# A state-space layer with gated feed-forward, forward and backward: gates by token rows, spectra formed in place, doubled table buffers, a shared transform pool, and another order and pace of the table chain

## Chip, core and metric

The kernel runs on one core of a Trainium2 chip. The metric is the device time of one execution in microseconds (us). "Span" is the profiled execution; it is some 2 us shorter than the time reported for it.

## The reference, cut

```python
def fwd(u, A, B, C, log_dt, Dskip, w1, w2):       # u: 2048 tokens x 512 channels, bf16
    xn = layernorm(u)
    dt = exp(log_dt)                              # per channel
    K  = einsum("dn,dnl,dn->dl", C, exp(dt*A*l), dt*B).real   # 128 states, complex; a kernel of 2048 taps per channel
    s  = irfft(rfft(pad(xn)) * rfft(pad(K)))[:2048] + xn * Dskip
    g  = silu(silu(xn @ w1) @ w2)                 # feed-forward 512 -> 1792 -> 512
    return u + s * g
# the outputs: fwd(...) and its gradients with respect to the 11 inputs, for a given grad_out
```

The channels are worked in four blocks of 128. For each block a *table* stage forms K (powers of exp(dt A) as sine times magnitude: E, Y, W, then ps_k, Xr, ps_e, KE). The code and the recorded texts count blocks from zero, so their "third block" is the fourth here. Long transforms are matmuls in two steps with a transposed load between: step one (ps_s from xn, Kb or ds, evacuated to dA), a transposing load dB<-dA, step two (ps_s from dB).

## The kernel before: the parts concerned

The kernel has generators that issue a few instructions and yield; a weaver takes steps from several in turn. So the place of a `yield` largely sets the order of instructions in every engine's queue (the build can still move one, as run 9 will show). The queues run in that order: compared by source line, VectorE ran its 1147 instructions of the kernel before, ScalarE its 673, and SP issued its 298 transfers, in the order of the built program.

```python
def dft_fwd(k, w8, U, X, ev):
    A = w8.tile(..., name="dA", tag="w8")
    ...                                    # step one: 32 matmuls, four evacuations to A
    yield
    B = w8.tile(..., name="dB", tag="w8")
    nc.sync.dma_start_transpose(B, A)      # the transposing load
    yield                                  # ONE step between issue and use
    ...                                    # step two: 16 matmuls on B, evacuated to a third tile X

def gen_conv_fwd(k, b):
    Kb = dft.tile(..., name="Kb", tag="t4")
    nc.sync.dma_start(Kb, k.Kd[b])         # the table stage's KE, back from memory; no step before its use
    yield from dft_fwd(k, dft, Kb, KX, k.evc)
    ...                                    # product with U, inverse transform, S_b
# gate (by 128-channel blocks), six operations on VectorE for each half block:
        nc.vector.tensor_scalar(out=th, in0=th, scalar1=-0.5, scalar2=0.5, ...)
        nc.vector.tensor_single_scalar(out=sl, in_=g, scalar=-1.0, op=ALU.add)
        ...
        nc.sync.dma_start(k.dSd[b][:, cs], fl(ds))      # d s goes to memory and back
# the program:
    def chain():
        yield from woven([gen_tables(k, 0), gen_conv_x(k, 0)], [5, 1])
        for b in range(1, 4):
            yield from woven([gen_tables(k, b), chained([gen_conv_fwd(k, b - 1), gen_conv_x(k, b)])], [3, 2])
    interleave_until([gen_ffn_fwd(k)], [1], ch)         # one chain step for each feed-forward step
    ...
    run(ch)                                             # what is left of the chain, alone
    fwd3 = gen_conv_fwd(k, 3); next(fwd3); run(pre(3)); run(fwd3); run(pre(0))
    interleave([gen_conv_bwd(k, 0), chained([post(0), pre(1), post(1), pre(2), post(2)])], [1, 2])
    interleave([chained(gen_conv_bwd(k, b) for b in range(1, 4)), gen_ffn_da(k, da)], [1, 2])
    interleave([gen_ssm_bwd(k, sb), chained([gen_dw2(k, fw), gen_dw1(k, fw)]), after(8, gen_ln_bwd(k, fw))], [2, 1, 1])
```

Of the kernel before, what the change touches and what calls it, by code (L numbers as in the profile page):

```python
# [18 lines left out]
PH = 1 << 18  # L19
# [67 lines left out]
def interleave_until(gens, weights, other):  # L87

    gens, weights = list(gens), list(weights)
    while gens:  # L90
        for i in range(len(gens) - 1, -1, -1):
            for _ in range(weights[i]):
                try:
                    next(gens[i])
                except StopIteration:
                    gens.pop(i); weights.pop(i)
                    break
        next(other, None)
# [15 lines left out]
def make_consts(k, wp):  # L114
# [24 lines left out]
    for h in range(2):  # L139
        hs = slice(8 * h, 8 * h + 8)  # L140
        prod = wp.tile([P, 8, 128], I32, name="prod", tag="prod", bufs=2)
        TT(out=prod[:], in0=il[:, hs].unsqueeze(2).to_broadcast([P, 8, 128]),
           in1=jf[:].unsqueeze(1).to_broadcast([P, 8, 128]), op=ALU.mult)
        ks = wp.tile([P, 8, 2, 128], I32, name="ks", tag="ks", bufs=2)
        TS(out=ks[:, :, 1, :], in_=prod[:], scalar=8191, op=ALU.bitwise_and)
        TS(out=prod[:], in_=prod[:], scalar=6144, op=ALU.add)
        TS(out=ks[:, :, 0, :], in_=prod[:], scalar=8191, op=ALU.bitwise_and)
        nc.scalar.activation(out=k.TF[:, hs], in_=ks[:], func=ACT.Sin, scale=2.0 * math.pi / 8192.0, bias=k.mpi[:])
# [112 lines left out]

def dft_fwd(k, w8, U, X, ev):

    nc, pc = k.nc, k.pc
    A = w8.tile([P, 2, 16, 16, 8], BF16, name="dA", tag="w8")
    for h in range(2):
        for c in range(2):
# [3 lines left out]
            ev(A[:, c, :, 8 * h:8 * h + 8, :], ps[:].rearrange("p t (g e) -> p g t e", e=8))  # L271
    yield
    B = w8.tile([P, 2, 16, P], BF16, name="dB", tag="w8")
    nc.sync.dma_start_transpose(B[:].rearrange("p c g k -> p (c g) k"), A[:].rearrange("p c g t e -> p (c g t e)"))
    yield
    F2 = k.F2
    for h in range(2):
        for c, (m0, m1) in enumerate(((0, 1), (2, 0))):
# [5 lines left out]
            ev(X[:, c, 8 * h:8 * h + 8, :], ps[:])  # L284


def dft_inv(k, w8, Y, ev, consume):
    nc, pc = k.nc, k.pc
    A2 = w8.tile([P, 2, 16, P], BF16, name="dA2", tag="w8")
# [17 lines left out]
def cplx_mul(k, w8, out, a, b, conj=False):  # L307
    nc = k.nc
    TT = nc.vector.tensor_tensor
    n = 8  # L310
    for g0 in range(0, 16, n):
        gs = slice(g0, g0 + n)
        t2 = w8.tile([P, 2, n, P], BF16, name="cm2", tag="cm2")
        TT(out=out[:, :, gs], in0=b[:, :, gs], in1=a[:, 0:1, gs].to_broadcast([P, 2, n, P]), op=ALU.mult)
        TT(out=t2[:, 0], in0=b[:, 1, gs], in1=a[:, 1, gs], op=ALU.mult)
        TT(out=t2[:, 1], in0=b[:, 0, gs], in1=a[:, 1, gs], op=ALU.mult)
        TT(out=out[:, 0, gs], in0=out[:, 0, gs], in1=t2[:, 0], op=ALU.add if conj else ALU.subtract)
        TT(out=out[:, 1, gs], in0=out[:, 1, gs], in1=t2[:, 1], op=ALU.subtract if conj else ALU.add)
# [22 lines left out]
def ssm_magnitudes(k, wp, S, ldt):  # L341
# [7 lines left out]
    nc.vector.scalar_tensor_tensor(out=ph[:], in0=k.dt[:], scalar=PH / (2 * math.pi), in1=S["Ai"], op0=ALU.mult, op1=ALU.mult)  # L349
    nc.vector.tensor_copy(out=qa_out(k.tau[:]), in_=qa_in(ph[:]))  # L350
    mag = wp.tile([P, 4, NE + len(Y_EXP), P], BF16, name="mag_all")
    for i, e in enumerate(E_EXP + Y_EXP):
        nc.scalar.activation(out=mag[:, :, i], in_=lamr[:].rearrange("p (b d) -> p b d", b=4), func=ACT.Exp, scale=float(e))
    for b in range(4):
# [23 lines left out]
def gen_tables(k, b):  # L378
# [4 lines left out]
    mag = tbl.tile([P, NX, P], BF16, name="mag", tag="mag")  # L383
    nc.sync.dma_start(mag[:].rearrange("p e d -> p (e d)"), k.Md[b])
    Xr = tbl.tile([P, 32, NE, 4], BF16, name="Xr", tag="Xr")
    for h in range(2):
        hs = slice(b * P + 64 * h, b * P + 64 * h + 64)
        ms = slice(64 * h, 64 * h + 64)
        E = tbl.tile([P, 2, 16, NE, 4], BF16, name="E", tag="E")
        Y = tbl.tile([P, 2, 16, 32, 4], BF16, name="Y", tag="Y")  # L390
        H = tbl.tile([P, 2, 16, 3, 4], BF16, name="H", tag="H")
        nc.gpsimd.memset(Y[:, 0, :, 0, :], 1.0)
        nc.gpsimd.memset(Y[:, 1, :, 0, :], 0.0)
        qe = lambda ap: ap.rearrange("p e (q a) -> p e q a", a=4)
        for (x0, n) in ((0, 8), (8, 8), (16, 5), (21, 7), (28, 3)):
# [4 lines left out]
            TS(out=V[:, 1, 0:n], in_=V[:, 1, 0:n], scalar=PH - 1, op=ALU.bitwise_and)  # L400
            TS(out=V[:, 0, 0:n], in_=V[:, 1, 0:n], scalar=PH // 4, op=ALU.add)
            TS(out=V[:, 0, 0:n], in_=V[:, 0, 0:n], scalar=PH - 1, op=ALU.bitwise_and)  # L402
            sn = tbl.tile([P, 2, 8, 64], BF16, name="sn", tag="ts", bufs=2)
            nc.scalar.activation(out=sn[:, :, 0:n], in_=V[:, :, 0:n], func=ACT.Sin, scale=-2 * math.pi / PH, bias=k.pi[:])  # L404
            for c in range(2):
# [4 lines left out]
                for o, s0, s1 in segs:  # L410
                    TT(out=o.rearrange("p q e a -> p e q a"), in0=qe(sn[:, c, s0:s1]), in1=qe(mag[:, x0 + s0:x0 + s1, ms]), op=ALU.mult)
# [14 lines left out]
        for q0 in range(0, 16, 8):  # L426
            W = tbl.tile([P, 4, 8, NE, 4], BF16, name="W", tag="W")
# [21 lines left out]
    KE = tbl.tile([P, 8, 8, 32], BF16, name="KE", tag="W")  # L449
# [31 lines left out]
def gen_conv_x(k, b):  # L481
# [3 lines left out]
    k.U = dft.tile([P, 2, 16, P], BF16, name="U", tag="w8")  # L485
    yield from dft_fwd(k, dft, lambda t: k.xn[:, t, bs], k.U, k.evc)
    k.nc.sync.dma_start(k.Ud[b], k.U[:].rearrange("p c g k -> p (c g k)"))
# [3 lines left out]
def gen_conv_fwd(k, b):  # L491
# [3 lines left out]
    U = k.U  # L495
    Kb = dft.tile([P, 4, 16, 32], BF16, name="Kb", tag="t4")
    nc.sync.dma_start(Kb[:].rearrange("p a t q -> p a (t q)"), k.Kd[b].rearrange("a i (r s) x -> (i r) a (s x)", s=2))
    KX = dft.tile([P, 2, 16, P], BF16, name="KX", tag="w8")
    yield from dft_fwd(k, dft, lambda t: Kb[:, :, t, :], KX, k.evc)
    nc.sync.dma_start(k.KXd[b], KX[:].rearrange("p c g k -> p (c g k)"))  # L500
    yield
    YX = dft.tile([P, 2, 16, P], BF16, name="YX", tag="w8")
    cplx_mul(k, dft, YX, KX, U)
    S = dft.tile([P, 16, P], BF16, name="S_b", tag="t4")

    def consume(t0, n, ps):
        xd = dft.tile([P, 8, P], BF16, name="xd", tag="xd")
        nc.vector.tensor_tensor(out=xd[:], in0=k.xn[:, t0:t0 + n, bs], in1=k.Dbc[:, bs].unsqueeze(1).to_broadcast([P, n, P]), op=ALU.mult)
        nc.vector.tensor_tensor(out=S[:, t0:t0 + n], in0=ps[:], in1=xd[:], op=ALU.add)
        if b in k.gate:  # L510
            gate_post(k, b, t0 // 8, S[:, t0:t0 + n])
    yield from dft_inv(k, dft, YX, k.evc, consume)
    if b not in k.gate:
        nc.sync.dma_start(k.Sd[b], S[:].rearrange("p t d -> p (t d)"))
# [4 lines left out]
def gen_ffn_fwd(k):  # L519
    nc, fp = k.nc, k.fp  # L520
    D, FT, DK, T = k.D, k.FT, k.DK, k.T
    for c in range(T // 2):
# [5 lines left out]
        for f in range(FT // 2):  # L528
            if f in (0, 4):
                hT = fp.tile([P, 8, 256], BF16, name="hT", tag="hT", bufs=3)  # L530
# [13 lines left out]
        ob = fp.tile([P, 4, 2, P], BF16, name="ob", tag="ob", bufs=2)  # L544
        for t in range(2):
# [4 lines left out]
            k.evf(ob[:, :, t, :], ps[:].rearrange("p (b d) -> p b d", b=4))  # L550
            yield
        k.st(k.Od[:, :, cs].rearrange("b p n -> p b n"), ob[:].rearrange("p b t d -> p b (t d)"))
# [3 lines left out]
def gen_gate_pre(k, b, pool):  # L556
# [3 lines left out]
    bs = slice(b * P, b * P + P)  # L560
    k.gate[b] = []
    for h in range(2):
        ts = slice(8 * h, 8 * h + 8)
        cs = slice(1024 * h, 1024 * h + 1024)
        n = dict(g=4, th=2, G=2, ds=1)
        g, th, G, ds = (pool.tile([P, 8, P], BF16, name=nm, tag=nm, bufs=n[nm]) for nm in ("g", "th", "G", "ds"))
        fl = lambda t: t[:].rearrange("p t d -> p (t d)")
        nc.sync.dma_start(fl(th), k.Od[b][:, cs])
        nc.sync.dma_start(G[:], k.g_v[:, ts, bs])
        x = None  # L570
        if b == 3:
            x = pool.tile([P, 8, P], BF16, name="x3", tag="x3", bufs=2)
            nc.sync.dma_start(x[:], k.x_v[:, ts, bs])
        nc.scalar.activation(out=g[:], in_=th[:], func=ACT.Silu)
        nc.scalar.activation(out=th[:], in_=th[:], func=ACT.Tanh, scale=0.5)
        TT(out=ds[:], in0=G[:], in1=g[:], op=ALU.mult)
        nc.sync.dma_start(k.dSd[b][:, cs], fl(ds))

        nc.vector.tensor_scalar(out=th[:], in0=th[:], scalar1=-0.5, scalar2=0.5, op0=ALU.mult, op1=ALU.add)
        sl = k.do[:, ts, bs]  # L580
        nc.vector.tensor_single_scalar(out=sl, in_=g[:], scalar=-1.0, op=ALU.add)
        TT(out=th[:], in0=sl, in1=th[:], op=ALU.mult)
        nc.vector.tensor_single_scalar(out=th[:], in_=th[:], scalar=1.0, op=ALU.add)
        TT(out=sl, in0=th[:], in1=G[:], op=ALU.mult)
        k.gate[b].append((g, x))
# [3 lines left out]
def gate_post(k, b, h, S, x=None):  # L589
# [3 lines left out]
    bs = slice(b * P, b * P + P)  # L593
    ts = slice(8 * h, 8 * h + 8)
    g, x3 = k.gate[b][h]
    x = x or x3
    TT(out=k.do[:, ts, bs], in0=k.do[:, ts, bs], in1=S, op=ALU.mult)
    TT(out=g[:], in0=g[:], in1=S, op=ALU.mult)
    TT(out=x[:], in0=x[:], in1=g[:], op=ALU.add)
    k.st(k.o0_v[:, ts, bs], x[:])  # L600


def gen_gate_post(k, b, pool):
    for h in range(2):
        S = pool.tile([P, 8, P], BF16, name="S", tag="S", bufs=1)
        x = pool.tile([P, 8, P], BF16, name="x", tag="x", bufs=1)
        k.nc.sync.dma_start(S[:].rearrange("p t d -> p (t d)"), k.Sd[b][:, 1024 * h:1024 * h + 1024])
        k.nc.sync.dma_start(x[:], k.x_v[:, 8 * h:8 * h + 8, b * P:b * P + P])
        gate_post(k, b, h, S[:], x)
# [3 lines left out]
def gen_conv_bwd(k, b):  # L613
# [3 lines left out]
    ds = dft.tile([P, 16, P], BF16, name="ds_b", tag="ds")  # L617
    nc.sync.dma_start(ds[:].rearrange("p t d -> p (t d)"), k.dSd[b])
    DS = dft.tile([P, 2, 16, P], BF16, name="DS", tag="w8")
    yield from dft_fwd(k, dft, lambda t: ds[:, t, :], DS, k.evc)  # L620
# [4 lines left out]
    GX = dft.tile([P, 2, 16, P], BF16, name="KGX", tag="w8")  # L625
    cplx_mul(k, dft, GX, U, DS, conj=True)

# [454 lines left out]
```

## Time and profile before

823.46 us, median of three runs (822.28 to 825.41). I follow a kernel by marks in the trace, each the start of an instruction:

| mark (us from the start) | before |
|---|---|
| last ps_o (end of the feed-forward forward) | 245.7 |
| last step-one matmuls from Kb (fourth block: all tables done) | 327.8 |
| first ps_da (feed-forward backward begins) | 377.9 |
| last ps_dx (feed-forward backward ends) | 575.0 |
| first matmul of G (gradients of the state space begin) | 586.7 |
| last psS (their last sums) | 778.6 |
| end of the span | 820.7 |

The page's strips, the stages, the waits and the thin stretch are shown in the prediction.

### The profile page before, as it was taken

The page shows a single profiled execution, that of the slowest core. Times are in us where ns is not written, and L with a number is a line of the kernel's source. Part 1 is how long each engine was busy: PE and PEld are TensorE (multiplying, and loading weights), DVE is VectorE, ACT ScalarE, POOL GpSimd, SP SyncE. Part 2 cuts the span into 40 slices and gives each one's busy share as a digit, 9 for nine tenths or more (in the row PEclk, how much of TensorE's full clock was granted, in tenths as well). Part 3 has the DMA queues.
Part 4 walks back from the last instruction along what each step waited for, and adds up shares of the span by engine and source line. Part 5 has one row for each costly group of instructions (what it writes and reads, how often), then busy time and mean ns, then how long its engine had stood idle before and what let it go on. Part 6 is the DMA issues. An engine that isn't in the chain of part 4 may idle for free. (4 is left out here: it accounts for less than half of the span.)

```text
span 820.7 us, 13722 instructions
## 1 busy us (share of the span) xinstructions
PE 606.2 (74%) x5356; PEld 419.0 (51%) x5356; DVE 545.3 (66%) x1163; ACT 490.3 (60%) x670; POOL 74.7 (9%) x163
## 2 busy tenths in 40 slices
PE   0678999777884572435688888889288778899986
PEld 0445565544643251122555656566155455578876
DVE  6989889635958874762866579495044367699640
ACT  6978777656863755532867476782165557775221
POOL 2011110001100000010000000000000001302221
PEclk9999999898996896676999999999779989899999
DMA  9995659635669789769476694856799999998363
GB/s 277 325 228 215 215 166 264 168 123 148 189 230 259 199 221 274 192 176 277 113 182 201 186 268 123 241 145 138 167 186 192 222 217 253 243 211 192 76 133 96
DMA packets 272257, 162.65 MB, mean 198 GB/s; under 512 B 204992, under 2 KB 254144, under 8 KB 269120
## 3 DMA queue, kind: packets, MB, share of 16 engines
q1 hardware_dynamic: 259216, 139.22, 68.1%
q0 software_dynamic: 6224, 18.10, 7.5%
q10 hardware_dynamic: 6752, 4.46, 1.7%
q8 instruction: 42, 0.69, 0.4%
q14 instruction: 23, 0.19, 0.1%
HBM read 51.77 MB, written 63.83 MB: 141 GB/s over the span
## 5 line engine op out<-in xcount | busy, mean ns | idle before, releaser
L535 PE MATMUL ps_h<-XT,W 128*128 128x256 bf16 x448 | 59.9, 283 | 29.9 <-DMA XT<-xn 25.8
L282 PE MATMUL ps_s<-dB,F 128*128 128x512 bf16 x96 | 44.6, 465 | 47.9 <-DMA dB<-dA 47.5
L887 PE MATMUL ps_w<-do,a_tok 128*128 128x512 bf16 x224 | 58.7, 408 | 15.6 <-ACT a_tok L884 15.6
L717 DVE TENSOR_TENSOR Tp<-Vb,Eb 128x1344 bf16<-128x1344 bf16 x64 | 52.5, 853 | 22.7 <-issue 9.2
L535 PEld LDWEIGHTS <-W 128*128 128x128 bf16 x448 | 43.5, 101 | 40.4 <-issue 19.6
L42 ACT CAST dA<-ps_s 128x1024 bf16<-128x1024 f32 x48 | 46.0, 1019 | 28.5 <-PE ps_s L270 28.4
L548 PE MATMUL ps_o<-W,aT 128*128 128x512 bf16 x224 | 57.5, 397 | 6.0 <-ACT hT L42 4.3
L861 PE MATMUL ps_da<-doT,W2T 128*128 128x256 bf16 x448 | 55.1, 273 | 2.2 <-DVE dhT L863 2.1
L905 PE MATMUL ps_w<-dh_tok,xn 128*128 128x256 bf16 x448 | 52.6, 273 | 2.2 <-DMA dh_tok<-DHd 2.2
L42 ACT CAST dA<-ps_i 128x1024 bf16<-128x1024 f32 x48 | 46.1, 1012 | 12.2 <-PE ps_i L294 11.1
L872 PE MATMUL ps_dx<-W1T,dhT 128*128 128x512 bf16 x224 | 51.8, 379 | 1.0 <-DVE dhT L863 1.0
L431 DVE TENSOR_TENSOR W<-E,CT 128x672 bf16<-128x672 bf16 x64 | 29.4, 503 | 33.0 <-DMA Kd<-KE 19.4
L861 PEld LDWEIGHTS <-W2T 128*128 128x128 bf16 x448 | 43.7, 98 | 10.1 <-issue 3.3
L270 PEld LDWEIGHTS <-TF 128*128 128x128 bf16 x384 | 27.6, 107 | 38.8 <-DMA Kb<-Kd 18.7
L863 DVE SCALAR_TENSOR_TENSOR dhT<-dhT,ps_da 128x512 bf16<-128x512 bf16 x56 | 36.6, 684 | 15.9 <-PE ps_da L861 15.6
L905 PEld LDWEIGHTS <-xn 128*128 128x128 bf16 x448 | 42.7, 98 | 7.7 <-issue 3.1
L42 ACT CAST Vb<-ps_v 128x672 bf16<-128x672 f32 x64 | 42.7, 723 | 6.4 <-PE ps_v L707 5.0
L884 ACT ACTIVATE a_tok<-a_tok 128x2048 bf16<-128x2048 bf16 x14 | 26.7, 1910 | 33.1 <-DMA a_tok<-Hd 33.1
L283 PE MATMUL ps_s<-dB,F 128*128 128x512 bf16 x96 | 44.1, 460 | 0.0
L436 PE MATMUL ps_k<-W,Y 128*128 128x84 bf16 x512 | 30.6, 206 | 17.8 <-DVE W L431 10.4
L404 ACT ACTIVATE sn<-V,pi 128x1024 bf16<-128x1024 int32 (+3 forms) x40 | 37.9, 967 | 9.5 <-DVE V L402 9.3
L887 PEld LDWEIGHTS <-a_tok 128*128 128x128 bf16 x224 | 22.0, 103 | 39.8 <-ACT a_tok L884 16.8
(233 smaller groups left out, 1378.4 us busy)
## 6 DMA issues: line engine op xcount, KB each, us to landing
Yd<-Y SPq DMA_DIRECT2D x8, 1024.0 KB, 4.9
Ed<-E SPq DMA_DIRECT2D x8, 672.0 KB, 3.5
Eb<-Ed SPq DMA_DIRECT2D x8, 672.0 KB, 5.6
Hd<-hT POOLq DMA_DIRECT2D x8, 512.0 KB, 6.1
Ud<-U SPq DMA_DIRECT2D x4, 1024.0 KB, 3.9
KXd<-KX SPq DMA_DIRECT2D x4, 1024.0 KB, 5.3
sp_in<-Ud SPq DMA_DIRECT2D x4, 1024.0 KB, 6.8
sp_in<-KXd SPq DMA_DIRECT2D x4, 1024.0 KB, 8.7
```

The source lines that it names most:

```text
L42: return self.nc.scalar.copy(out=out, in_=in_)
L282: nc.tensor.matmul(out=ps[:, 4 * u:4 * u + 4], lhsT=F2[:, m0], rhs=B[:, 0, g0:g0 + 4, :], start=True, stop=False)
L283: nc.tensor.matmul(out=ps[:, 4 * u:4 * u + 4], lhsT=F2[:, m1], rhs=B[:, 1, g0:g0 + 4, :], start=False, stop=True)
L404: nc.scalar.activation(out=sn[:, :, 0:n], in_=V[:, :, 0:n], func=ACT.Sin, scale=-2 * math.pi / PH, bias=k.pi[:])
L535: nc.tensor.matmul(out=ps[:, j], lhsT=k.W1[:, dk, ft * P:ft * P + P], rhs=XTv[:, :, dk, :], start=(dk == 0), stop=(dk == DK - 1))
L548: nc.tensor.matmul(out=ps[:], lhsT=aT[:, ft, t * P:t * P + P], rhs=k.W2[:, ft, :], start=(ft == 0), stop=(ft == FT - 1))
L717: k.nc.vector.tensor_tensor(out=Tp[:, r, :, c].rearrange("p q w e a -> p q w (e a)"), in0=Vb[:, :, c], in1=Eq[:, ec].unsqueeze(2).to_broad ...
L861: nc.tensor.matmul(out=ps[:, j], lhsT=W2T[:, dk, ft * P:ft * P + P], rhs=dTv[:, :, dk, :], start=(dk == 0), stop=(dk == DK - 1))
L863: nc.vector.scalar_tensor_tensor(out=dh[:, i0:i0 + 2, :], in0=dh[:, i0:i0 + 2, :], scalar=1.0, in1=ps[:], op0=ALU.add, op1=ALU.mult)
L872: nc.tensor.matmul(out=ps[:], lhsT=dhs[ft // 8][:, ft % 8, t * P:t * P + P], rhs=k.W1T[:, ft, :], start=(ft == 0), stop=(ft == FT - 1))
L887: nc.tensor.matmul(out=ps[:], lhsT=a[:, t, :], rhs=k.do[:, t, :], start=(t == 0), stop=(t == k.T - 1))
L905: nc.tensor.matmul(out=ps[:], lhsT=k.xn[:, t, dk * P:dk * P + P], rhs=dh[:, t].rearrange("p j n -> p (j n)"), start=(t == 0), stop=(t == k ...
```

## The change

Its intent: keep TensorE supplied between the feed-forward forward and its backward. The gates are done by token rows, which leaves d s on chip, with two of their one-input operations on POOL. Products of spectra are formed in place, one transform pool serves forward and backward. E and W get two buffers, KE its own, Y two tiles that are initialised once. The chain of tables goes at 1.6 steps for each feed-forward step, and its inner order changes: three steps instead of one behind each transposing load, three behind the load of Kb, and the two convolution parts side by side.

```diff
-def dft_fwd(k, w8, U, X, ev):
+LAG = 3
+def dft_fwd(k, w8, U, ev, tag="w8"):
 ...
-    yield
     B = w8.tile(...); nc.sync.dma_start_transpose(B, A)
-    yield
+    for _ in range(LAG):
+        yield
 ...                                       # step two is evacuated into A again
     nc.sync.dma_start(Kb, k.Kd[b])
-    yield from dft_fwd(k, dft, Kb, KX, k.evc)
+    for _ in range(LAG):
+        yield
+    KX, A2 = yield from dft_fwd(k, dft, Kb, k.evc)
+    U = spectrum_in(k, dft, b, "U")       # the spectrum of u, back from memory
 ...
-        E = tbl.tile(..., tag="E")
+        E = tbl.tile(..., tag="E", bufs=2)
-            W = tbl.tile(..., tag="W")
+            W = tbl.tile(..., tag="W", bufs=2)
-    KE = tbl.tile(..., tag="W")
+    KE = tbl.tile(..., tag="KE")
 ...                                       # gate, by rows of two tokens per partition
+        nc.gpsimd.tensor_scalar(out=o, in0=o, scalar1=-0.5, scalar2=0.5, ...)
+        nc.gpsimd.tensor_scalar(out=g[:], in0=g[:], scalar1=1.0, scalar2=-1.0, ...)
 ...
-        yield from woven([gen_tables(k, 0), gen_conv_x(k, 0)], [5, 1])
+        yield from woven([gen_tables(k, 0), gen_conv_x(k, 0)], [2, 1])
-            yield from woven([gen_tables(k, b), chained([gen_conv_fwd(k, b - 1), gen_conv_x(k, b)])], [3, 2])
+            yield from woven([gen_tables(k, b), gen_conv_x(k, b), gen_conv_fwd(k, b - 1)], [3, 1, 1])
-        interleave_until([gen_ffn_fwd(k)], [1], ch)
+    paced(gen_ffn_fwd(k), ch, 1.6)
 ...
+    run(woven([gen_gate_rows(k, gp), gen_conv_fwd(k, 3)], [1, 1]))
+    interleave([chained(gen_conv_bwd(k, b) for b in range(4)), gen_ffn_da(k, da), after(12, gen_out(k, da))], [1, 2, 1])
```

## The prediction

Sum: 823.5 - 28 - 37 + 24 - 6, given as 769.5, rounded to 770 (it is 776.5). In the gap's term the 2.7 us for a row group is the estimate; the times of its four VectorE operations in the trace of before sum to 2.5.

> **What bounds the kernel now.** I read the page first, then cut the span into its stages with the windows view, then asked the waits of VectorE, and last the timeline of TensorE where it is thin. The busy strips of the page:
>
> ```profile
> PE   0678999777884572435688888889288778899986
> DVE  6989889635958874762866579495044367699640
> ACT  6978777656863755532867476782165557775221
> PEclk9999999898996896676999999999779989899999
> ```
>
> No engine is busy throughout; a slice is 20.5 us. TensorE is near full from slice 4 to 11, again from 20 to 27, and from 29 on. Between, in slices 12 to 19, it falls to 2 to 5 tenths and its granted clock falls too. Cut by stages (the first figure of each pair is busy us):
>
> ```profile
> core 0: us, PE busy (x) PEld busy (x) DVE busy (x) ACT busy (x) POOL busy (x), PEclk, DMA share, GB/s
> 26.00:246.00 220.00, 183.94 (x1477) 117.11 (x1476) 164.78 (x405) 160.04 (x226) 25.00 (x39) 0.94 0.69 204
> 246.00:311.00 65.00, 37.78 (x333) 23.90 (x330) 49.51 (x95) 36.86 (x59) 1.90 (x4) 0.84 0.90 228
> 311.00:402.00 91.00, 38.23 (x264) 24.70 (x265) 56.46 (x91) 43.30 (x48) 7.86 (x8) 0.68 0.77 204
> 402.00:578.00 176.00, 151.54 (x1224) 105.65 (x1223) 123.85 (x177) 108.16 (x109) 1.47 (x3) 0.99 0.70 186
> 578.00:600.00 22.00, 5.72 (x31) 3.95 (x31) 3.03 (x2) 4.81 (x4) 0.00 (x0) 0.61 0.85 176
> 600.00:821.00 221.00, 188.74 (x2029) 143.39 (x2029) 128.77 (x340) 118.46 (x194) 32.48 (x57) 0.94 0.86 183
> ```
>
> Row by row: feed-forward with part of the table chain beside it (TensorE 84% busy); the rest of the table chain alone (58%); the third-block forward transform, the gates and the first backward transform (42%, clock 0.68); the three other backward transforms with the feed-forward backward (86%); a changeover (26%); the parameter gradients with the weight gradients (85%). So 178 us of the span, from 246 to 402 and from 578 to 600, hold 81.7 us of TensorE work, some at a lowered clock. There the time is set by chains of latency, not by an engine. The waits that show this:
>
> ```profile
> DVE KGX L314 <- DMA sp_in<-Ud: 32.3, 4, 21.4
> DVE W L431 <- DMA Kd<-KE: 19.4, 3, 17.3
> DVE W L431 <- PE ps_k L436: 13.6, 5, 8.0
> ```
>
> The first: VectorE stood 21.4 us once until a stored spectrum came back for the first backward product. The second and third: the table product W has a single buffer, which KE shares, so VectorE waited for the stores of KE and for the matmuls that read W. And the thin stretch in order of time:
>
> ```profile
> 324.05 1.89 PE L270 MATMUL ps_s<-Kb,TF 128*128 128x128 bf16 x16 [14.58 <-DMA Kb<-Kd]
> ...
> 338.40 0.61 PE L282 MATMUL ps_s<-dB,F 128*128 128x512 bf16 x1 [10.28 <-DMA dB<-dA]
> ...
> 352.94 1.95 PE L303 MATMUL ps_i<-dA,TI 128*128 128x128 bf16 x32 [1.25 <-ACT dA L42]
> ...
> 372.80 0.61 PE L282 MATMUL ps_s<-dB,F 128*128 128x512 bf16 x1 [11.63 <-DMA dB<-dA]
> ```
>
> That is one forward transform from 324 to about 360, then one backward transform, each with nothing beside it on TensorE. The feed-forward backward runs steadily only from about 402.
>
> [...]at 338 to 344 the 512-column matmuls start 0.43 us apart, at 305 to 309 0.215 us.[...]
>
> **The change part by part.**
>
> Pace and buffers of the table chain. Before, the chain takes one step per feed-forward step (72), and about a quarter of it is left over. After, it takes 1.6 per step, 115 for some 111 steps, so all of it but the last block's forward transform lies beside the feed-forward; the built instruction order confirms it: only one ps_i1 group of 32 matmuls stands after the last ps_o. W and E are doubled and KE has its own buffer, which removes up to 19.4 + 13.6 = 33 us of VectorE waits. The work of 26 to 311 is 183.9 + 37.8 = 221.7 us of TensorE, some 215 if the tail is at full clock. At the 84% reached from 26 to 246 that is 256 us, so this stage ends near 282 to 283 where it ended at 311. VectorE: 165 + 50, less about 15 of gates that lay in the tail, less the phase work (per 512-element group 684 + 3 x 420 ns become 684 + 420 + 684, 0.15 us, times 40 = 6 us): 194 of 257 us, 76%. ScalarE 160 + 37 less some 10 of gates, 187, 73%. Neither is the bound by itself. Saving: 28 us.
>
> The gap between. After the chain, the last forward transform still runs alone, 36 us as before (324 to 360), a start of a few us for Kb, and after it the last gate products (2 x 0.69), and the transposes of do: 3.5 us of issue plus about 4 to land. That alone is 47 us. Beside it stand the gate rows: VectorE per row group 688 + 688 + 469 + 688 = 2.5 us, eight times 20.3 (before 688 + 422 + 422 + 688 + 469 + 688 = 3.4, times 8 = 27.0), the products with S 8 x 0.69 = 5.5, and the transform's own 11.8 (spectrum product 1.22 + 4 x 0.69, twice; output 0.69 + 1.22, twice). 37.6 us of VectorE in 47, and in the built order six row groups stand before the spectrum product. They wait for the last Od store and its way back (4.4 + 5.4 us to landing), ScalarE (2.1 us a group) and POOL (two operations a group[...]). Six groups at 2.7 us after about 12 us put the product at +28 instead of +22. So 47 + 7 = 54 us to the feed-forward backward, against 402 - 311 = 91 before. Saving 37 us. The round trip of d s through memory and its waits (3.8 + 3.3 + 9.5 us) are gone with it, and the 21.4 us wait for the spectra, whose loads now come before.
>
> The backward stage gets longer: it takes over the first backward transform and the output. TensorE: 151.5 us were three transforms and nearly all of the feed-forward backward; a transform is about 15 us net, so 167. VectorE: a transform is 2 x 8.0 + 3.8 = 19.7 us, the rest 74, the output 8 x 2 x 0.69 = 11: 164. Before, 151.5 of TensorE took 176 (86%) at 70% of VectorE. 167 at 86% is 194; VectorE would then be at 85% and in-order bursts of 8 us will cost something: 200 us. Also each transform holds the only two w8b buffers until its end, so the four run in series at some 53 us each. Cost: 24 us.
>
> The changeover. In the built order 32 matmuls of ps_w2 (32 x 0.26 = 8 us) stand before the first matmul that needs the gradients of the kernel back. That fills part of the 22 idle us: I take 6 us.
>
> Sum: 823.5 - 28 - 37 + 24 - 6 = 769.5, rounded to 770.
>
> **The rivals.** First, that VectorE or ScalarE becomes the bound of the merged feed-forward and table stage, since three in-order engines at 73 to 84% do not overlap freely. For: from 140 to 180 VectorE was less than half busy while TensorE was 80% busy, so dependencies bite. Against: from 60 to 140 TensorE ran at 90% with VectorE at 87%. If it holds, the stage ends at 295 and the total is about 783.[...] Third, that the backward stage keeps its old pace per transform and VectorE does not limit: 190 us, and with a denser first stage (270) the total is near 748. Fourth, that a buffer that was cut (hT from 3 to 2, ob to 1, w8 from 5 to 4, with the spectrum of u read back) makes a new wait in the first stage; the landings of 4 to 7 us are short beside its 27 us per token block, so I give it 5 us at most. That nothing is won would need two of these at their worst together.
>
> **Range and chances.** The stage ends are uncertain by about 10 us in the first stage, 8 in the gap, 10 in the backward stage and 4 at the changeover; taken as independent, 17 us, or 22 for 8 in 10; a little more upward for unknown waits: 748 to 797. 2% is 16.5 us, so faster needs less than 807: chance 0.92; within 2% 0.06; slower 0.02.
>
> **What would show it.** The last ps_o near 283 and few matmuls of the tables after it; TensorE 84% or more from 26 on; the first dhT with ps_da near 337 and no single VectorE wait of 20 us;[...] the last ps_dx near 537; gradients then as long as before, less some 6 us. Wrong would be: table matmuls long after the last ps_o, W waiting for ScalarE or for stores again,[...] or the backward stage past 215 us.

## The result, and the profile after

The changed kernel took 787.3 us, median of four (783.09 to 791.35); the kernel before 822.87 (821.77 to 825.41) beside it. The ratio is 0.956, 95% interval 0.951 to 0.962. A ratio here is the mean time of one kernel's fast runs over that of the other's of the same rounds, so it is not quite the ratio of the medians. Later the same kernel, unaltered, gave 779.9 and 0.945 (0.939 to 0.951). The two ratios of one kernel thus differ by 1.1%. I therefore read smaller differences from marks in the traces and not from totals.

One thing about the prediction before its steps are judged. Its sum has a slip: 823.5 - 28 - 37 + 24 - 6 is 776.5 and not 769.5. Its own marks say the same: 283, 337, 537, then 16 and 221 us, end of the span at 774. So 7 of the 17 us by which 770 fell short are arithmetic. Below, "predicted" is the working.

| mark | before | predicted | after | after, run again |
|---|---|---|---|---|
| last ps_o | 245.7 | 283 | 266.8 | 263.5 |
| last step one from Kb | 327.8 | | 280.4 | 277.3 |
| first ps_da | 377.9 | 337 | 340.8 | 338.2 |
| last ps_dx | 575.0 | 537 | 531.1 | 528.3 |
| first G | 586.7 | 553 | 553.6 | 550.0 |
| last psS | 778.6 | | 741.6 | 732.6 |
| end of span | 820.7 | 774 | 789.5 | 778.0 |

The strips of the page after:

```profile
PE   0479987889999623579889789994787788788985
DVE  6979988598599149949689587964442675698510
ACT  6869767588698274638646477645474667663111
PEclk9979998999999855679899899997699899999999
```

The thin stretch of eight slices (12 to 19) has become some four, from slice 13. By stages (busy us first in each pair):

```profile
core 0: us, PE busy (x) PEld busy (x) DVE busy (x) ACT busy (x) POOL busy (x), PEclk, DMA share, GB/s
26.00:267.00 241.00, 212.04 (x1752) 137.25 (x1775) 193.82 (x423) 185.07 (x280) 21.52 (x29) 0.94 0.83 238
267.00:341.00 74.00, 25.64 (x177) 16.06 (x177) 52.26 (x65) 39.25 (x38) 20.48 (x17) 0.58 0.92 274
341.00:532.00 191.00, 173.06 (x1329) 120.31 (x1342) 147.31 (x208) 117.78 (x123) 6.89 (x12) 0.94 0.77 209
532.00:554.00 22.00, 10.12 (x33) 3.86 (x35) 8.84 (x30) 10.96 (x17) 2.30 (x4) 0.70 0.95 215
554.00:790.00 236.00, 188.49 (x2018) 148.05 (x2026) 124.62 (x314) 112.76 (x180) 29.90 (x53) 0.92 0.82 169
```

Feed-forward and tables together take 241 us with TensorE 88% busy (212.04 of 241). The gap takes 74 us at a clock of 0.58 and now has 20 us of POOL work in it. The changeover takes 22 us although TensorE does 10 us of work there. The gap in TensorE's timeline:

```profile
276.65 1.89 PE L270 MATMUL ps_s<-Kb,TF 128*128 128x128 bf16 x16 [7.72 <-DMA Kb<-Kd]
...
294.00 0.61 PE L282 MATMUL ps_s<-dB,F 128*128 128x512 bf16 x1 [13.29 <-DMA dB<-dA]
...
312.45 0.61 PE L295 MATMUL ps_i<-I,sp_in 128*128 128x256 bf16 x2 [7.07 <-DVE sp_in L318]
...
340.84 4.43 PE L854 MATMUL ps_da<-doT,W2T 128*128 128x256 bf16 x20 [8.27 <-DMA doT<-do]
```

This is one forward transform alone, as predicted. But its first matmul comes 10 us after the last ps_o, and from there to ps_da it is 64 us. Over the whole gap TensorE waits three times for a load (Kb, dB, doT) and once for VectorE (the spectrum product).

### The profile page after: what moved, and what is told of

Its sections match the earlier page's. It is cut to its first block, busy times and chain, and to the rows that moved or that the text cites. A ratio compares the mean times of both kernels' runs of the same rounds, so it can differ in the third digit from the quotient of the medians.

```text
span 789.5 us, 13610 instructions
## 1 busy us (share of the span) xinstructions
PE 609.8 (77%) x5305; PEld 426.0 (54%) x5356; DVE 545.8 (69%) x1107; ACT 484.5 (61%) x670; POOL 87.1 (11%) x167
## 4 chain that ended last, share of the span: by engine, by line
PE 21%; DVE 17%; DMA 15%; ACT 8%; issue 7%; SPq 6%; POOL 1%; ACTq 0%; POOLq 0%; DVEq 0%
DMA a_tok<-Hd 5%; PE ps_da L854 3%; PE ps_i L295 3%; PE ps_dx L865 2%; DMA go_g<-gd 2%; PE ps_w L880 2%; PE ps_v L700 2%; PE ps_e L447 2%; DMA Pd<-pd_s 1%; PE G L669 1%; DVE dhT L856 1%; ACT dB L42 1%; PE psS L719 1%; PE psS L723 1%; DMA GE<-dKd 1%
## 5 line engine op out<-in xcount | busy, mean ns | idle before, releaser
L42 ACT CAST dA<-ps_s 128x1024 bf16<-128x1024 f32 x96 | 94.1, 1034 | 43.9 <-PE ps_s L270 22.8
L854 PE MATMUL ps_da<-doT,W2T 128*128 128x256 bf16 x448 | 62.0, 297 | 16.8 <-DMA doT<-do 8.3
L710 DVE TENSOR_TENSOR Tp<-Vb,Eb 128x1344 bf16<-128x1344 bf16 x64 | 52.3, 850 | 25.0 <-ACT Vb L42 13.6
L880 PE MATMUL ps_w<-do,a_tok 128*128 128x512 bf16 x213 | 54.4, 403 | 18.4 <-ACT a_tok L877 17.9
L42 ACT CAST dB<-ps_i 128x1024 bf16<-128x1024 f32 x48 | 47.3, 1019 | 33.0 <-PE ps_i L295 26.2
L295 PE MATMUL ps_i<-I,sp_in 128*128 128x256 bf16 x384 | 54.6, 290 | 14.1 <-DVE sp_in L318 10.4
L854 PEld LDWEIGHTS <-W2T 128*128 128x128 bf16 x448 | 47.5, 107 | 26.9 <-issue 16.3
L282 PE MATMUL ps_s<-dB,F 128*128 128x512 bf16 x95 | 39.6, 417 | 27.1 <-DMA dB<-dA 21.5
L295 PEld LDWEIGHTS <-sp_in 128*128 128x128 bf16 x384 | 38.2, 103 | 31.9 <-DVE sp_in L318 13.6
L700 PE MATMUL ps_v<-Gb,YT 128*128 128x168 bf16 x256 | 31.2, 261 | 14.5 <-ACT Vb L42 7.9
L42 ACT CAST o<-ps_w 128x256 bf16<-128x256 f32 (+1 forms) x42 | 18.4, 439 | 38.6 <-PE ps_w L898 37.3
L270 PEld LDWEIGHTS <-TF 128*128 128x128 bf16 x384 | 26.6, 103 | 23.3 <-issue 11.9
```

Source lines behind the costliest of these rows:

```text
L42: return self.nc.scalar.copy(out=out, in_=in_)
L282: nc.tensor.matmul(out=ps[:, 4 * u:4 * u + 4], lhsT=F2[:, m0], rhs=B[:, 0, g0:g0 + 4, :], start=True, stop=False)
L295: nc.tensor.matmul(out=ps[:, g], lhsT=Y[:, c, g0 + g, :], rhs=k.I2[:, c].rearrange("p c m -> p (c m)"), start=(c == 0), stop=(c == 1))
L700: nc.tensor.matmul(out=ps[:, u, 168 * c:168 * c + 168], lhsT=YT[:, c, q + u, :], rhs=Gb[:, q0 + q + u].rearrange("p w x -> p (w x)"), star ...
L710: k.nc.vector.tensor_tensor(out=Tp[:, r, :, c].rearrange("p q w e a -> p q w (e a)"), in0=Vb[:, :, c], in1=Eq[:, ec].unsqueeze(2).to_broad ...
L854: nc.tensor.matmul(out=ps[:, j], lhsT=W2T[:, dk, ft * P:ft * P + P], rhs=dTv[:, :, dk, :], start=(dk == 0), stop=(dk == DK - 1))
```

## The experiments

All twelve gave correct results; "run 4" further on means the fourth of this list. The kernel before: 818.2 us (runs 1, 2, 7 and 8), 824.2 (runs 3, 4, 9 and 10), 823.1 (runs 5, 6, 11 and 12).

### 1. Pace 1 again

```diff
-    paced(gen_ffn_fwd(k), ch, 1.6)
+    paced(gen_ffn_fwd(k), ch, 1.0)
```

> One part undone: one step of the table chain goes with each step of the feed-forward again, instead of 1.6. The last feed-forward store (ps_o) then comes early and the chain ends alone, as in the kernel before. Theory (the first stage is shorter because TensorE work lies beside the whole chain): the first stage ends 15 to 28 us later than the 267 us of the changed kernel, its last part has TensorE about half busy, the total is 800 to 815 us. Rival (the doubled tables, not the pace, gave the 44 us): the stage ends within 5 us of 267 and the total stays within 5 us of 787.

785.8 us, ratio 0.959 (0.952 to 0.965). The last ps_o came at 208.9 already, and the chain went on alone behind it, yet the last step one from Kb stood at 285.2 (280.4 in the changed kernel) and the first ps_da at 340.3. My theory fell: the pace by itself gives 5 us at that mark and nothing at the next.

### 2. One buffer each for E and W again

```diff
-        E = tbl.tile(..., tag="E", bufs=2)
+        E = tbl.tile(..., tag="E", bufs=1)
-            W = tbl.tile(..., tag="W", bufs=2)
-    KE = tbl.tile(..., tag="KE")
+            W = tbl.tile(..., tag="W", bufs=1)
+    KE = tbl.tile(..., tag="W", bufs=1)
```

> One part undone: the E and W table tiles have one buffer each again and KE shares W's, all else as in the changed kernel. Theory (VectorE's waits of 19.4 and 13.6 us for W went with the second buffer): the waits for W come back, and the first stage ends 8 to 20 us later than 267, the total at 795 to 807 us. Rival (with the pace at 1.6 the waits are covered by feed-forward work): waits for W show, but the stage ends within 4 us of 267 and the total within 5 us of 787.

780.1 us, ratio 0.951 (0.945 to 0.958). Last step one from Kb at 277.7, first ps_da at 337.4. VectorE's waits for W summed to 1.4 us, where the kernel before had 33. The rival holds: with the pace at 1.6 the second buffers do nothing, and the waits of 19.4 and 13.6 us which I had credited to them went for another reason.

### 3. Both undone together

Edits 1 and 2 in one kernel.

> Both undone together: pace 1 and one buffer each for E and W (KE shares W's). Singly neither moved the end of the tables: the last first-step matmul of the third block's transform (ps_s from Kb) starts at 280 in the changed kernel, at 285 with pace 1, at 278 with one buffer, and at 328 in the kernel before. Theory C (either the pace or the buffers is enough, as each hides what the other removes): together they bring most of the 43 us back, that matmul starts at 310 to 328 and the total is 810 or more at a kernel before of 818. Theory D (neither matters; something else in the chain was changed): it starts at 278 to 292, the total stays at 780 to 788.

800.1 us, ratio 0.974 (0.966 to 0.982), so against the limit of 2% the class is unclear. Last step one from Kb at 321.2. Waits for W are back (12.7 us for ps_k, 3.9 for KE's store). So at that mark theory C is right: either the pace or the buffers is enough, and the loss of both is 41 us, where the losses singly were 5 and -3. The expected 810 was not reached. The first ps_da came only 38 us behind the mark, not 60, since the gate rows were further on by then; 19 us of loss were left at ps_da.

### 4. The chain's old order, at pace 1

```diff
-LAG = 3
+LAG = 1
-    yield from woven([gen_tables(k, 0), gen_conv_x(k, 0)], [2, 1])
+    yield from woven([gen_tables(k, 0), gen_conv_x(k, 0)], [5, 1])
-        yield from woven([gen_tables(k, b), gen_conv_x(k, b), gen_conv_fwd(k, b - 1)], [3, 1, 1])
+        yield from woven([gen_tables(k, b), chained([gen_conv_fwd(k, b - 1), gen_conv_x(k, b)])], [3, 2])
-    paced(gen_ffn_fwd(k), ch, 1.6)
+    paced(gen_ffn_fwd(k), ch, 1.0)
```

> The chain's order of before with all else of the changed kernel: the two convolution parts one after the other at two steps for three of the tables, one step instead of three after the issue of each transposed load, none after the load of Kb, and pace 1. To be compared with the run of pace 1 alone (last ps_o at 209, last first-step matmul from Kb at 285, 786 us). Theory D1 (the steps put between a load and its use, and the two convolution parts side by side, gave the first stage its gain): that matmul starts at 305 to 330, the total is 800 to 820, and TensorE and VectorE wait for dB and Kb as in the kernel before. Theory D2 (two Y tiles that are set once, KE's own buffer and less VectorE work gave it, not the order): it starts at 280 to 292, the total is within 6 us of 786.

825.8 us, ratio 1.005 (0.996 to 1.014), with the mark at 322.9: theory D1, with a total 6 us above its range. With the order of before nothing is left of the gain, with both tables doubled, d s on chip and the gates by rows.

### 5. The old order at pace 1.6

Edit 4 without its last two lines.

> The chain's order of before (as in the run of the old order, 826 us) but with the pace at 1.6, so that the whole chain lies beside the feed-forward. Theory E (pace, buffers and order are substitutes: a chain that lies beside feed-forward matmuls hides its own waits, so with pace 1.6 the order is worth little): the last first-step matmul from Kb starts at 280 to 296, and the total is within 10 us of the changed kernel's. Theory F (the order is worth what it gave at pace 1, as the feed-forward is held up in the same in-order queues while the chain waits for dB and Kb): that matmul starts at 305 or later, the total is 20 us or more above the changed kernel's.

823.7 us, ratio 1.001 (0.995 to 1.007); last step one from Kb at 319.2. Theory F. The last ps_o came at 283.1, which is the predicted end of the merged stage to the microsecond: I had worked it out from the TensorE share of before, and this kernel has the order of before. But behind it the fourth block's transform of u and the end of the tables still stood alone, 36 us to the mark (14 in the changed kernel), so even there the stage did not deliver. Part of the 36 is a queue: the transposing load of W2T held SP's queue from 302.0 to 311.4, and the load of Kb was issued right after it.

### 6. The lag alone, at pace 1

```diff
-LAG = 3
+LAG = 1
-    paced(gen_ffn_fwd(k), ch, 1.6)
+    paced(gen_ffn_fwd(k), ch, 1.0)
```

> Pace 1 and one step instead of three between the issue of a transposed load and its use, and after the load of Kb; the convolution parts stay side by side with the tables at 3, 1, 1. To be compared with pace 1 alone (Kb's last first step at 285, 786 us) and with the old order at pace 1 (323, 826 us). If the lag is what the order gives: 310 to 325 and 805 to 826 us, with TensorE waiting longer for dB and Kb than the 7.1 and 5.8 us of pace 1 alone. If it is that the two convolution parts stand side by side: within 6 us of pace 1 alone.

826.6 us, ratio 1.002 (0.996 to 1.008); mark at 322.2, last ps_o at 247.4 (208.9 with lag 3 at the same pace). The lag is what the order gives: 37 us at the mark against run 1. LAG also sets how many steps the chain has (by the `yield`s 111 with lag 3, 91 with lag 1), so at pace 1 the 72 feed-forward steps take 79% of it with them instead of 65%, which delays the last ps_o. That doesn't explain the later mark, where all tables are done: with lag 3 a larger share, at pace 1.6, moved it by 5 us only, and to earlier. The two stages compare best between the starts of KE's stores, one per block, which are 103.1, 150.0, 206.8 and 262.2 us in the changed kernel and 101.9, 169.6, 238.6 and 305.9 here. The windows view of the changed kernel, cut there (the columns are those of the stages above):

```profile
103.00:150.00 47.00, 39.78 (x322) 24.78 (x324) 37.76 (x75) 32.04 (x54) 2.29 (x3) 0.89 0.72 214
150.00:207.00 57.00, 50.36 (x437) 33.30 (x443) 44.22 (x87) 45.01 (x68) 4.01 (x5) 0.94 0.86 246
207.00:262.00 55.00, 50.58 (x463) 34.08 (x468) 42.05 (x81) 46.08 (x72) 4.57 (x6) 1.00 0.83 241
```

and of the kernel with lag 1:

```profile
102.00:170.00 68.00, 57.06 (x502) 38.35 (x500) 46.37 (x90) 48.50 (x74) 4.58 (x6) 0.97 0.68 196
170.00:238.00 68.00, 59.02 (x492) 38.25 (x491) 48.10 (x95) 48.85 (x73) 5.49 (x7) 0.92 0.65 213
238.00:306.00 68.00, 40.24 (x317) 25.06 (x316) 35.03 (x63) 31.66 (x52) 1.39 (x2) 0.85 0.61 190
```

A block takes 68 us in place of 47 to 57; in the kernel before the first and the last store are 205 us apart, also 68 a block on average. From 26 us to the last store TensorE is idle for 60 of 280 us with lag 1 (busy 220.3) and 29 of 236 (busy 207.1) in the changed kernel. No single wait holds the difference. Between the same marks the waits that the trace names for TensorE sum to 57 against 27 us, for ScalarE to 92 against 53, for VectorE to 65 against 36. TensorE's longest groups with lag 1 are hT behind ScalarE (11.9), sp_in behind VectorE (9.4) and Kb (9.3). The expectation was half right here: up to the mark TensorE waits longer for Kb (23.4 us, 7.1 in run 1) but not for dB (1.9, 5.8 in run 1; the expectation names the two figures the other way round). The runs show that the lag does it and that the waits are spread; in what way it spreads them is not shown. Which of its places (behind dB or behind Kb) counts for how much was not tried, nor was it separated whether the time to land counts or that more steps spread a transform's matmuls over more of the next tables.

### 7. The gate's one-input operations on VectorE

```diff
-        nc.gpsimd.tensor_scalar(out=o, ...)
-        nc.gpsimd.tensor_scalar(out=g[:], ...)
+        nc.vector.tensor_scalar(out=o, ...)
+        nc.vector.tensor_scalar(out=g[:], ...)
```

> The two one-input operations of each gate pair of rows go from POOL back to VectorE: 16 operations of about 0.42 us, 6.7 us more VectorE work. Theory A (POOL holds the gap up: VectorE's two-input operations beside it take 1.52 us instead of 0.68, and POOL's 1.0 to 1.5 us lie in the chain): VectorE's mean in the gap falls back to about 0.7 us, and the gap from the last ps_o to the first ps_da falls from 74 to 60 to 67 us, the total to 774 to 782 us. Theory B (the gate's loads, its stores and the in-order queue of ScalarE hold the gap up): the gap stays within 4 us of 74 and the total within 5 us of 787.

770.6 us, ratio 0.941 (0.935 to 0.948). First ps_da at 331.3, gap 65 us: theory A. By groups in the gap, the changed kernel (after "|" the busy us and the mean ns of one):

```profile
L571 POOL TENSOR_SCALAR g<-g 128x1024 bf16<-128x1024 bf16 x8 | 10.0, 1258 | 5.3 <-DMA gd<-g 3.3 <-DVE ds L567 1.3 <-POOL g L571 0.7
...
L572 DVE TENSOR_TENSOR do<-do,g 128x1024 bf16<-128x1024 bf16 x8 | 7.9, 992 | 3.8 <-POOL g L571 3.8
```

and this run:

```profile
L572 DVE TENSOR_TENSOR do<-do,g 128x1024 bf16<-128x1024 bf16 x8 | 5.5, 685 | 0.0
...
L571 DVE TENSOR_SCALAR g<-g 128x1024 bf16<-128x1024 bf16 x8 | 3.4, 422 | 1.3 <-DMA gd<-g 1.3
```

The 1.52 us of the expectation is the longest of the changed kernel's eight products, whose median is 682 ns. The same product takes 685 ns instead of 992 once POOL is silent (0.57 us of work in 65.5, against 20.48 in 74). So 16 more operations left VectorE busy for 46.5 us in the gap instead of 52.3.

### 8. Eight g buffers

```diff
-        g = gp.tile(..., tag="g", bufs=3)
+        g = gp.tile(..., tag="g", bufs=8)
-    k.W1T = da.tile(...)                      # the space comes from here
+    k.W1T = pool("da1", ...).tile(...)        # opened after the gate stage
```

> The gate's g tile has eight buffers instead of three (the space comes from W1T, which is placed after the gate stage; its load is later anyway). Nothing else changes. Theory B (ScalarE stands in its queue behind a g buffer that the store to gd and the product still hold, so that the inverse transform's evacuations come 1 to 3 us late): ScalarE's waits of 3.75 and 2.96 us for g go, and the gap falls from 74 to 64 to 70 us, the total to 775 to 783 us. Theory A (VectorE and POOL set the pace of the gate, buffers only show it): the waits move to the next reader, the gap stays within 4 us of 74 and the total within 5 us of 787.

780.9 us, ratio 0.953 (0.947 to 0.958), first ps_da at 342.6, so the gap did not shorten. ScalarE's 7.4 us of waits for g are gone, and TensorE's wait for the spectrum product grew from 7.1 to 15.5 us: unthrottled, the gate rows ran ahead of it on VectorE, and beside a denser POOL (its operations took 1315 and 1431 ns on average) their product took 1202 ns. By the gap it is theory A again; the wait moved. The total lies in theory B's range and below theory A's, but since the unaltered kernel later gave 779.9 us, it decides nothing.

### 9. The parameters' transposed loads after those of GE

```diff
-    par = load_params(k, sb, 0, k.D)          # six transposing loads at the start of gen_ssm_bwd
 ...
             vb[i] = ssm_v(...)
+            if i == 0:
+                par = load_params(k, sb, 0, k.D)
```

> The six transposed loads of the parameters, which the changed kernel issues from SP between 539 and 547 and ahead of the four loads of GE, are issued after those. Theory (the changeover got no shorter because the queue holds GE back): GE is issued about 8 us earlier, from the last ps_dx to the first G takes 12 to 16 us instead of 22, the total falls by 5 to 9 us to 774 to 778 at a kernel before of 818. Rival (the SSM stage then waits for the next thing, YT or Eb or the zeroing matmul behind ps_w2): the first G comes earlier, the last psS does not, and the total stays within 3 us of 783.

781.0 us, ratio 0.949 (0.942 to 0.956). SP's timeline in the kernel before:

```profile
569.36 1.19 SPq L327 DMA_TRANSPOSE par_Ar<-in_A_A_re_dram  x1
...
579.30 1.35 SPq L658 DMA_DIRECT2D GE<-dKd  x2
...
592.26 4.64 SPq L883 DMA_TRANSPOSE a_tok<-Hd  x2
```

in the changed kernel:

```profile
527.76 3.65 SPq L876 DMA_TRANSPOSE a_tok<-Hd  x1
...
532.13 3.09 SPq L876 DMA_TRANSPOSE a_tok<-Hd  x1
...
538.98 1.60 SPq L331 DMA_TRANSPOSE par_Ar<-in_A_A_re_dram  x1
...
547.14 2.67 SPq L651 DMA_DIRECT2D GE<-dKd  x4
```

and in this run:

```profile
537.27 2.83 SPq L651 DMA_DIRECT2D GE<-dKd  x4
```

GE is issued 10 us earlier; from the last ps_dx to the first G it takes 14 us, not 22. In the changed kernel the six loads held SP's queue for 1.26 to 1.60 us each there; larger transposing loads held it longer, those of dB 4.75 to 8.44 us and that of W2T 7.65 (6.90 in run 1, 13.16 in run 2). But the parameters' loads stood ahead of GE in the kernel before as well, beside the last of the feed-forward backward. What is new ahead of them are the loads for the weight and layer-norm gradients (a_tok, du, Gt and pd_l, on SP from 527.8 to 539.0), although the program names these later: the build moved them. This run left them where they are. The last psS comes at 730.6, where the changed kernel has 741.6 and 732.6 in its two profiles. So the theory holds for the changeover. How much of it reaches the end of this run its total does not show: it lies between the two measurements of the unaltered kernel.

### 10. Two weight-gradient steps instead of one

```diff
-    interleave([gen_ssm_bwd(...), chained([gen_dw2(...), gen_dw1(...)]), ...], [2, 1, 1])
+    interleave([gen_ssm_bwd(...), chained([gen_dw2(...), gen_dw1(...)]), ...], [2, 2, 1])
```

> Last stage only: two steps of the weight gradients instead of one with each two steps of the SSM gradients. In the kernel before and in the changed one alike, 288 of the 448 dw1 matmuls stand after the last psS, and the end comes 42 and 48 us after it. Theory (that tail is TensorE work alone and can lie beside the SSM chain, which is not TensorE-bound): the tail after the last psS falls to 20 to 30 us, the stretch from the first G to it grows by less than half of what the tail loses, the total falls by 8 to 20 us to 763 to 775 at a kernel before of 818. Rival (the stage is bound by TensorE, as I had it in the prediction): the stretch grows by as much as the tail loses, and the total stays within 5 us of 783.

793.5 us, ratio 0.965 (0.957 to 0.973). My theory fell. The tail behind the last psS shrank from 48 (45 run again) to 21 us, and the stretch from the first G to it grew from 188 (183) to 218, with the changeover 5 us longer too (27.9 for 22.5). The windows from the first G on, changed kernel:

```profile
554.00:742.00 188.00, 153.94 (x1726) 119.43 (x1735) 114.85 (x276) 105.12 (x161) 22.36 (x41) 0.92 0.91 187
742.00:790.00 48.00, 34.55 (x295) 28.62 (x292) 9.78 (x38) 7.64 (x20) 7.54 (x12) 0.93 0.46 98
```

and this run:

```profile
557.00:776.00 219.00, 185.50 (x2004) 144.56 (x2004) 124.31 (x304) 114.54 (x189) 26.75 (x47) 0.90 0.85 180
776.00:797.00 21.00, 1.95 (x8) 0.67 (x8) 9.77 (x38) 0.96 (x2) 3.71 (x7) 0.57 0.03 9
```

TensorE works 82% of the time in the first stretch of the changed kernel and 85% here: 32 us of matmuls moved in lengthened it by 31 us. In this run more matmuls did not fill the idle 18%, and what remains at the end is the chain of the last block's gradients, with no matmuls left beside it.

### 11. The changed kernel again

> The changed kernel unaltered, on the chip of this call, so that the three runs beside it are compared on one chip. Every theory expects a ratio of 0.950 to 0.962 to the kernel before, the last first-step matmul from Kb at 278 to 282, and the first ps_da at 338 to 342.

779.9 us, ratio 0.945: below the range I gave, though its interval of 0.939 to 0.951 reaches into it. The marks are in the table above. Up to the first G they stand 3 us earlier throughout, the end 11.5.

### 12. Edits 7 and 9 together

> The two parts that helped, together: the gate's one-input operations on VectorE, and the parameters' transposed loads after those of GE. They lie in different stages, so the savings of 9 us in the gap (first ps_da at 331) and 8 us at the changeover (first G 14 us after the last ps_dx) should add: a ratio of 0.930 to 0.942 to the kernel before, some 14 to 20 us below the changed kernel on the same chip. If one of the two only moved a wait to a later stage, as the weight-gradient steps did: 5 to 10 us below it.

770.1 us, median of six, ratio 0.9345 (0.930 to 0.939), against 779.9 and 0.945 for the changed kernel: 10 us less. The ratio lies in the range expected; the difference is at the upper end of what the theory of a pure shift expects and short of the 14 to 20 of the sum. First ps_da at 329.6 (338.2 in the run beside it), first G 15 us after the last ps_dx (22), end of the span at 764.4 (778.0). The stretch from the first G to the last psS took 189 us where the other took 183: some of the gain was given back there. It has the lowest ratio. Its gain over run 7, which has only the first of the two edits, is not shown: that took 770.6 us on the same chip, and the two ratios' intervals overlap. They were run at other times.

## Why the prediction was right, and where not

**The first stage: shorter than predicted, for another cause.** The step "so this stage ends near 282 to 283" came out at 266.8. It took the saving from the pace and from the doubled buffers and assumed that TensorE's share of 84% would stay. Runs 1 to 3 show that pace and buffers are substitutes: each alone is dispensable, both missing cost 41 us at the mark. Runs 4 and 5 show that both together are worth little with the chain's old order (319.2 at the mark), and run 6 that at pace 1 the lag is what counts in that order. The term that the working lacked is the lag, a constant of 3 in the diff, which lifts TensorE's share to 88% and takes the block from 68 to 47 to 57 us. I had read the diff for what it does to tiles and had not asked what three yields do to the queues. Run 5, which is nearest to the prediction's own assumption (TensorE 82% busy to the last ps_o), ended the feed-forward at 283.1, and gained nothing in all.

**The gap: 54 us predicted, 74 found.** Three terms were too small. "A start of a few us for Kb" is 10 us from the last ps_o (276.65 - 266.8): Kb's load stands in SP's queue behind the load of W2T (until 268.4) and the store of S_b, which waits for VectorE; it is issued at 271.9 and takes 4.8 us to land. And the gate rows in front of the spectrum product: I had named POOL as a rival, but put in 7 us for the whole of it. POOL's operations took 1.26 us on average, and VectorE's product beside them 992 ns against 688 for such a product in the kernel before. Taking POOL out gave 9 us (run 7); more buffers gave none (run 8). With the start's excess of some 8 us, if "a few" is 2, this is 17 of the 20 us. The other 3 fit the wait for dB (13.3 us, where the kernel before had 10.3): ScalarE now does six operations of the gate between the evacuations of dA; no run tested this. And the saving of 37 us in this step was largely one of bookkeeping. It set the gap's end at 402 for the kernel before, where the feed-forward backward "runs steadily", but the first ps_da stood at 377.9. From the end of the tables, 311, to there it is 67 us, so by its own marks the gap grew by 7 us.

**The backward stage: 200 predicted, 190 found.** The third rival's figure was the right one. VectorE is 77% busy there (147.3 of 191), not the 85% that I feared, and TensorE keeps 91% (173.1 of 191).

**The changeover and the gradients: 237 predicted, 258 and 250 found.** This is the step that was furthest off. I took the window from 578 to 600 as a changeover of 22 us and expected 32 matmuls of ps_w2 to fill 6 of them. In the trace of before the first G came at 586.7, 12 us after the last ps_dx, and the rest of that window belonged to the gradients. The 32 matmuls do stand there now, but the changeover waits for GE and not for TensorE, and it grew to 22 us. The parameters' loads ahead of GE take 8 us of it (run 9), but they stood there before too; new ahead of GE are 11 us of loads for the weight and layer-norm gradients. That these made it grow is read from the queue and was not tested. The premise behind the credit, that matmuls moved forward into a wait shorten the end, did not come true. Run 10 shows that matmuls added beside the gradients take time one for one, but the 32 that left that stretch saved nothing measurable: from the first G to the end it took 234 us before, 236 and 228 after.

Taken together for the first measurement: -16, +20, -10 and +21 us against the working's marks, 15 in all, and 774 becomes 789. The class was right because these errors nearly cancel: 15 us is less than the 33 between 774 and the 807 needed. That is luck in good part, as is the close agreement of the marks from 337 to 553 with 340.8 to 553.6: two errors of opposite sign cancel in it. By the marks of the first table the kernel gains 47 us up to the last step one from Kb and loses 16 behind it (10 to the first ps_da, 11 at the changeover, 2 to the end, and 7 won between). So the whole gain lies in the first stage, and the working had left out the constant without which, at pace 1, there is none (run 6).

## What to carry to other kernels

When generators are woven into the engines' queues, the number of steps between issuing a load and using it is a part of the change like any buffer: here, at pace 1, one constant decided over the whole gain, while the buffers or the pace could be taken away singly at next to no cost. Test parts of a change in pairs as well as singly, because substitutes hide each other. And a stage's border should be a named instruction in the trace, not a round number of a window.
